# Attention stage of a three-part kernel: third key buffers, an exponential in another place, zero rows written after the first gated tile, maxima turned by a transposition

## The chip, the cores and the metric

The kernel runs on one core of a Trainium2 chip. That core has five engines that run their own instruction streams and meet by semaphores: TensorE (PE, matrix products; PEld is its weight load), VectorE (DVE), ScalarE (ACT), GpSimd (POOL) and SyncE (SP), which here only issues DMA transfers. The metric is the device time of one execution in microseconds, lower is better.

## The reference

Three parts follow each other; the output of one is the input of the next. All values are fp32, and the kernel keeps that accuracy by splitting an operand into a rounded high part and the rest.

```python
# 1: attention, batch 4, 8 heads, 576 positions, 64 wide
scores = q @ k.T / sqrt(64);  cum = cumsum(log(clip(f, 1e-4, 1)))
scores = where(causal, -1e9, scores + cum[:, None] - cum[None, :])
attn = exp(scores - max(scores));  attn /= sum(attn) + 1e-9
x = (attn @ v), heads side by side            # 2304 x 512
# 2: gated product
x = (((x @ w1) * (x @ w2)) @ w3) @ w_out      # 512 -> 1024 -> 1024 -> 512
# 3: one of 8 experts for each row
logits = x @ w_gate;  e = argmax(logits)
gate = softmax(logits)[e];  eom = sigmoid(x @ w_output_gate)
out[rows of e] = gate * eom[e] * (relu(x @ w1[e]) @ w2[e])
```

## The kernel before

Attention goes by 16 tiles of two heads each (four batches of four pairs). A tile passes through some 55 small stages: load of queries, keys and values (`lq`, `lk`, `lv`), rounding of both to a high part on ScalarE (`qh`, `kh`, line 212), the rest of both on VectorE (`ql`, `kl`, line 219), scores from the high parts alone (`X0` to `X3`, `XL`, line 226) for the row maxima on VectorE (`m0` to `mL`, line 261), the turn of the maxima from a column into a row (`Tm`, line 270), its copy (`tc`) and its spread over partitions by two DMA transfers (`mv`, tile MR), the exact scores in four groups A to D (`GA` to `HD`), the exponentials (`eA` to `eD`, line 300), causal masks and sums on GpSimd (`a0` to `s3`, lines 306 and 318), the product with the values (`p0` to `p3`, line 327), the row sums (`su`) and the output copy (`xa`). Rows of the cumulated decay (tile CK) come by DMA (`ck`), and the sums go to DRAM, are inverted there by batches and are read back as a broadcast (`xl`, tiles rb).

The order of all this is written out by hand. `START` gives each stage a time within the tile, `PERIOD` (9.8) the distance of two tiles, `SHIFT` exceptions for single tiles; all (stage, tile) pairs are sorted by that time, and instructions are recorded in that order. Each engine then takes its own in that order and waits where something is not ready. The numbers set an order only, no times. So in one stretch of time stages of three or four tiles are mixed: while GA to GD of tile n run, the values' product is that of tile n - 1, and the first scores are those of tile n + 2. All loads and stores of the stage stand on one queue, SP's.

Between the attention stages, the steps `c0` to `c6` convert weights of the second part (`Combined.narrow`, lines 474 to 492: load, one op on ScalarE, three on VectorE, a rounding on ScalarE, a subtraction on GpSimd). PSUM has three two-bank buffers for all score tiles (`pss`), which rotate; a product waits until its buffer's last reader is through.

The third part scatters each row of its input into a DRAM table `xs`, 2304 rows for each expert; before, 384 rows of each expert must have been cleared (`cr`, line 381), since not all of them are written. In the second part, tile 0 of 512 rows goes through `gated(0)`; then rows of tile 1 are split (`xsplit(1)`), the gates' weights (wg) are loaded, and `project(0)` follows, whose gates' product reads wg (line 682) and whose rows are scattered by GpSimd (line 738).

Lines that matter below:

```python
zt = st["zt"] = p3.tile([P, DM + 2], F32, name="zero", bufs=1)   # tile 2 of attention
SP.dma_start(out=xs[e * N:e * N + W]..., in_=...)                # tiles 4 to 11, one expert each
PE.matmul(s["t"], Ms[s["n"] % 2], ident, start=True, stop=True)  # line 270
SP.dma_start(out=wg[:, :, :2 * E], in_=gates)                    # line 823
```

Of the kernel before, what the change touches and what calls it, by code (L numbers as in the profile page):

```python
# [11 lines left out]
F32 = mybir.dt.float32  # L12
F32R = mybir.dt.float32r
# [10 lines left out]
NP = H // 2  # L24
N = B * S
DM = H * D
FF = 1024
E = 8
P = 128
# [3 lines left out]
W = 3 * P  # L33
# [14 lines left out]

PERIOD = 9.8
START = {  # L50
# [8 lines left out]
}  # L59
SHIFT = {(0, "qd"): -2.0, (0, "lq"): 7.41, (1, "lk"): 0.5, (1, "lq"): 0.5, (0, "XL"): -4.55, (0, "mL"): -5.9, (0, "Tm"): -1.8, (0, "tc"): -1.8, (0, "mv"): -3.49, (1, "Tm"): -0.1, (1, "tc"): -0.1}  # L60

FILL = {(0, "XL"): 10, (1, "X0"): 1, (0, "HA"): 1, (0, "HB"): 3, (1, "XL"): 3, (2, "X0"): 2}

# [7 lines left out]
def spread(nc, d, rz):  # L71

    for h in range(2):
        nc.sync.dma_start(out=d[64 * h:64 * h + 64], in_=rz[h:h + 1].broadcast_to([64, rz.shape[1]]))


def attention(nc, tc, ident, xT, rz, xs, wc, q, k, v, f):
# [6 lines left out]
    V, A, G, PE, SP = nc.vector, nc.scalar, nc.gpsimd, nc.tensor, nc.sync  # L84
    with (
# [7 lines left out]
        p2 = inputs.enter_context(tc.tile_pool(name="at2", bufs=2, side="right"))  # L93
# [22 lines left out]
        CKs = [p1.tile([P, 640], F32R, name=f"CK{i}") for i in range(3)]  # L116
        MRs = [p1.tile([P, S], F32R, name=f"MR{i}") for i in range(2)]
        OQ, OD = p1.tile([P, P], F32R, name="OQ"), p1.tile([P, P], F32R, name="OD")
        KHs = [[p2.tile([P, 640], F32R, name=f"{x}{i}", bufs=1) for i in range(2)] for x in ("kh", "kl")]
        QDs = [p1.tile([P, P], F32R, name=f"QD{i}") for i in range(2)]  # L120
        Ms = [p1.tile([P, 64], F32, name=f"M{i}") for i in range(2)]
        tri, tril = p1.tile([P, 640], F32, name="tri"), p1.tile([P, S], F32, name="tril")
# [57 lines left out]
        st = {}  # L180

        def tl(s, key, shape, dt=F32, bufs=2):
            if key in ("kh", "kl"):
                s[key] = KHs[key == "kl"][s["n"] % 2]
                return s[key][:, :S]
            if key not in s:
                pool = p2 if key in ("qr", "kr", "kh", "kl", "qh", "ql") else p3
                s[key] = pool.tile([P, *shape], dt, name=f"{key}_{s['n']}", tag=key, bufs=bufs)
            return s[key]
# [4 lines left out]
        def load(s, x):  # L194
            n = s["n"]
            src, shape = {"q": (q, (S,)), "k": (k, (S,)), "v": (v, (5, P))}[x]
            SP.dma_start(out=tl(s, x + "r", shape), in_=src[n // NP, n % NP])

        def decay(s):
            n = s["n"]  # L200
# [10 lines left out]
        def high(s, x):  # L211
            A.activation(out=tl(s, x + "h", (S,), F32R), in_=s[x + "r"], func=ACTF.Copy)
# [54 lines left out]
        def turn(s):  # L267
            x = st[s["n"] + 1]["x", 1][:, 256:] if 1 < s["n"] < B * NP - 1 else s["x", 4][:, 896:]
            s["t"] = x[0:64, :P]
            PE.matmul(s["t"], Ms[s["n"] % 2], ident, start=True, stop=True)  # L270

        def turned(s):
            A.activation(out=tl(s, "mt", (P,), F32R)[0:9], in_=s["t"][0:9], func=ACTF.Copy)
# [104 lines left out]
                else:  # L378
                    G.tensor_tensor(out=xT[:, i, 0:512], in0=xT[:, i, 0:512], in1=d, op=ALU.mult)

        def clear_rows(s):

            e = s["n"] - 4
            if e == -2:
                zt = st["zt"] = p3.tile([P, DM + 2], F32, name="zero", bufs=1)
                G.memset(zt, 0.0)
                G.memset(zt[:, DM + 1:], float(2 * N))
            if 0 <= e < E:
                SP.dma_start(out=xs[e * N:e * N + W].rearrange("(c p) d -> p c d", p=P), in_=st["zt"].unsqueeze(1).broadcast_to([P, W // P, DM + 2]))

        stages = {
            "ck": (decay,), "qd": (last_queries,), "XL": (scores_last,), "mL": (maxima, 4), "Tm": (turn,), "tc": (turned,), "mv": (spread_maxima,),
            "p0": (pv, (0,)), "p1": (pv, (1, 2)), "p3": (pv, (3, 4)), "su": (sums,), "xa": (weighted,), "sa": (keep_sums,),
            "zs": (store_sums,), "rl": (invert, 0), "ra": (invert, 1), "rv": (invert, 2), "rs": (invert, 3), "cr": (clear_rows,), "xl": (first_tile, 0), "xm": (first_tile, 1),
        }
        for x in "qkv":
            stages["l" + x] = (load, x)
# [11 lines left out]
        for n in range(B * NP):  # L409
            st[n] = {"n": n}  # L410
        order = [(START[x] + SHIFT.get((n, x), 0.0) + PERIOD * n, n, i, x) for n in range(B * NP) for i, x in enumerate(START)]
        order = sorted(order + [(t + PERIOD * (B * NP - 1), B * NP, 0, x) for x, t in AFTER.items()])
# [132 lines left out]
def moe(nc, tc, ident, xT, rz, xs, xpool, raws, region, wc, w1, w2, gates, e1, e2, out):  # L545

    V, A, G, PE, SP = nc.vector, nc.scalar, nc.gpsimd, nc.tensor, nc.sync
    NCH = N // P
    with (
# [5 lines left out]
        st = {"work": wc.work, "unit": 1}  # L555
# [10 lines left out]
        def tmp(name):  # L566
            return st["work"].tile([P, 512], F32, name=name, tag="tmp", bufs=TMP if "moa" in st else 3)

        def split(src, hi, lo, lo_eng):
            G.tensor_scalar(out=hi, in0=src, scalar1=1.0, scalar2=1.0, op0=ALU.mult, op1=ALU.mult)  # L570
            lo_eng.tensor_tensor(out=lo, in0=src, in1=hi.bitcast(F32), op=ALU.subtract)
# [11 lines left out]
        def xparts(t):  # L583
            return [st["moa"].tile([P, 4, 512], F32R, name=f"{x}{t}", tag=x) for x in ("xh", "xl")]

        def xsplit(t, w, x, ks=range(4)):
            xh, xl = x
            for k in ks:
                xv = xT[:, k, 512 * t:512 * t + w]
                if t:  # L590
                    d = tmp(f"rz{t}{k}")[:, :w]
                    spread(nc, d, rz[k, :, 512 * t:512 * t + w])
                    G.tensor_tensor(out=xv, in0=xv, in1=d, op=ALU.mult)  # L593
                if t:
                    split(xv, xh[:, k, :w], xl[:, k, :w], V)
                else:
                    A.activation(out=xh[:, k, :w], in_=xv, func=ACTF.Copy)
                    V.tensor_tensor(out=xl[:, k, :w], in0=xv, in1=xh[:, k, :w].bitcast(F32), op=ALU.subtract)
# [190 lines left out]
        for hf, j in wc.steps:  # L789
# [4 lines left out]
            if hf and j == 5:  # L794
                wc.first.close()
                st["moa"] = xpool.enter_context(tc.tile_pool(name="moa", bufs=1, side="right", reuse_waits="tile"))
                x = xparts(0)
# [18 lines left out]
        gated(0, TT[0], x, iter(()))  # L816
        x = xparts(1)
        xsplit(1, TT[1], x)


        wg = p1.tile([P, 4, 32], F32, name="wg")
# [26 lines left out]
        with tc.manual_schedule(engines={PE_E, POOL_E}):  # L848
            for t, w in list(enumerate(TT))[1:]:
# [3 lines left out]
                if t + 1 < len(TT):  # L853
                    x = xparts(t + 1)
# [295 lines left out]
        with tc.manual_schedule(engines={PE_E, DVE_E}):  # L1150
# [40 lines left out]
            x = next(fx)  # L1191
# [12 lines left out]
            for i in range(1, E):  # L1204
# [18 lines left out]
                x = next(fx, None)  # L1223
# [9 lines left out]
                else:  # L1233
                    x = turned_piece("p", g2)
                    take(y)
                    p = piece("p", ws2, g2, x)
# [8 lines left out]
        with tc.For_i(1, npieces, 1) as s:  # L1245
            e = nc.values_load(tab[0:1, bass.ds(s + E, 1)], engines=SPE, min_val=0, max_val=E - 1)
# [58 lines left out]
```

## Time and profile before

| | us |
|---|---|
| median of 3 runs | 792.49 |
| lowest, highest run | 791.95, 793.69 |
| profiled execution | 791.35 |
| its span, first to last instruction | 789.7 |
| TensorE busy in the span | 769.1 (97%) |
| VectorE busy | 447.4 (57%) |
| GpSimd busy | 315.9 (40%) |
| ScalarE busy | 280.2 (35%) |

Attention takes the first 173 us or so, the combination of w3 with w_out and the gated product the time to 550 us, the experts the rest. The granted clock of TensorE is 0.996 of full speed as a mean. A row of the timeline gives start, duration, engine, line, operation, and the tiles written and read (buffer numbers left out); in brackets stands how long the engine was idle just before, and what ended that. SPq is SP's instruction stream: its rows are the issues of transfers, not their data. A TensorE row's end is modelled, since matmuls overlap.

### The profile page before, as it was taken

The numbers are of one execution on the slowest core, as the hardware profiler recorded it, in microseconds if no ns is written. First come the engines' busy times: TensorE is split into PE (matmuls) and PEld (weight loads), VectorE is DVE, ScalarE is ACT, GpSimd is POOL, SyncE is SP. The second block draws the span as 40 slices with busy tenths as digits, with TensorE's granted clock in tenths as the row PEclk, the third lists the DMA queues.
The fourth block names the chain that finished last, engine by engine and source line by source line (L and its number), as shares of the span: only waits on it lengthen the run. The fifth ranks groups of instructions, "written<-read, shape, count | busy, mean of one in ns | idle before, by whom it ended". The sixth has DMA issues, their size and how long they took to land. (4 is left out here: it accounts for less than half of the span.)

```text
span 789.7 us, 13796 instructions
## 1 busy us (share of the span) xinstructions
PE 769.1 (97%) x5142; PEld 646.0 (82%) x5142; DVE 447.4 (57%) x982; ACT 280.2 (35%) x542; POOL 315.9 (40%) x343
## 2 busy tenths in 40 slices
PE   7999999999999999999999999999999999999995
PEld 3677777777888887887888788898797999999983
DVE  7689988978989604332350422347468735545620
ACT  3566666654556222212212221214221222322221
POOL 6679999991000501130230111033454444545420
PEclk9999999999999999999999999999999999999998
DMA  3557777534643111010100000054677456456460
GB/s 97 175 164 234 233 234 238 148 115 140 194 152 134 54 42 41 27 40 15 54 16 4 35 27 0 14 169 139 214 240 227 145 204 226 136 189 214 142 268 30
DMA packets 40211, 102.12 MB, mean 129 GB/s; under 512 B 8610, under 2 KB 9314, under 8 KB 39888
## 3 DMA queue, kind: packets, MB, share of 16 engines
q1 hardware_dynamic: 36960, 91.46, 36.0%
q0 software_dynamic: 3184, 9.77, 3.2%
q8 instruction: 41, 0.67, 0.3%
q14 instruction: 26, 0.21, 0.1%
HBM read 84.47 MB, written 16.51 MB: 128 GB/s over the span
## 5 line engine op out<-in xcount | busy, mean ns | idle before, releaser
L607 DVE TENSOR_TENSOR ga<-b,ga 128x512 f32<-128x512 f32 (+1 forms) x40 | 25.4, 635 | 144.4 <-PE b L579 143.7
L738 POOL DMA_INDIRECT xs<-xr,pos x18 | 19.5, 1083 | 174.3 <-DVE pos L732 126.6
L261 DVE CUSTOM_DVE_ANT_0 junk<-x,tri 128x256 f32<-128x256 f32 (+3 forms) x128 | 62.8, 491 | 15.0 <-PE x L226 5.5
L577 PE MATMUL h<-gh,ah 128*128 128x320 f32 (+4 forms) x224 | 67.2, 300 | 0.0
L578 PE MATMUL h<-gl,ah 128*128 128x320 f32 (+4 forms) x224 | 66.9, 299 | 0.0
L579 PE MATMUL h<-gh,al 128*128 128x320 f32 (+4 forms) x224 | 66.9, 299 | 0.0
L577 PE MATMUL b<-xh,w2h 128*128 128x512 f32 (+1 forms) x160 | 59.9, 375 | 0.0
L577 PE MATMUL a<-xh,w1h 128*128 128x512 f32 (+1 forms) x160 | 59.8, 374 | 0.0
L579 PE MATMUL a<-xh,w1l 128*128 128x512 f32 (+1 forms) x160 | 58.9, 368 | 0.0
L579 PE MATMUL b<-xh,w2l 128*128 128x512 f32 (+1 forms) x160 | 58.9, 368 | 0.0
L578 PE MATMUL a<-xl,w1h 128*128 128x512 f32 (+1 forms) x160 | 58.8, 368 | 0.0
L578 PE MATMUL b<-xl,w2h 128*128 128x512 f32 (+1 forms) x160 | 58.8, 368 | 0.0
L577 PE MATMUL y<-raw,gh 128*128 128x512 f32 x144 | 56.8, 395 | 0.0
L579 PE MATMUL y<-raw,gl 128*128 128x512 f32 x144 | 56.2, 390 | 0.0
L578 PE MATMUL y<-raw,gh 128*128 128x512 f32 x144 | 56.0, 389 | 0.0
L609 ACT ACTIVATE gh<-ga 128x512 fp32r<-128x512 f32 (+1 forms) x40 | 23.5, 589 | 89.3 <-DVE ga L607 89.3
L570 POOL TENSOR_SCALAR bh<-rb 128x1024 fp32r<-128x1024 f32 x28 | 35.9, 1283 | 46.1 <-DMA rb<-e 40.6
L1031 DVE SCALAR_TENSOR_TENSOR hl<-h,hh 128x320 fp32r<-128x320 f32 (+4 forms) x56 | 25.5, 462 | 47.9 <-ACT hh L1030 47.2
L593 POOL TENSOR_TENSOR xT<-xT,rz 128x512 f32<-128x512 f32 (+1 forms) x16 | 21.4, 1336 | 78.0 <-DVE ga L607 78.0
L327 PE MATMUL v<-PT,vr 128*64 128x448 f32 (+4 forms) x384 | 52.4, 394 | 0.0
L306 POOL TENSOR_SCALAR_AFFINE_SELECT PT<-PT 128x256 f32<-128x256 f32 (+1 forms) x80 | 42.6, 554 | 22.9 <-ACT PT L300 21.2
L318 POOL TENSOR_TENSOR ac<-ac,PT 128x640 f32<-128x640 f32 (+1 forms) x32 | 47.7, 1490 | 1.6
(617 smaller groups left out, 2120.7 us busy)
## 6 DMA issues: line engine op xcount, KB each, us to landing
ra<-e SPq DMA_DIRECT2D x28, 512.0 KB
rb<-e SPq DMA_DIRECT2D x28, 512.0 KB
w<-w3t SPq DMA_DIRECT2D x16, 512.0 KB
xs<-zero SPq DMA_DIRECT2D x8, 771.0 KB
vr<-v SPq DMA_DIRECT2D x16, 320.0 KB
kr<-k SPq DMA_DIRECT2D x16, 288.0 KB
qr<-q SPq DMA_DIRECT2D x16, 288.0 KB
wo<-wo SPq DMA_DIRECT2D x8, 512.0 KB
```

The costliest lines, as they stand in the source:

```text
L261: V.tensor_tensor_reduce(out=junk[:, :w], in0=s["x", i][:, 512 * h:512 * h + w] if i < 4 else s["x", i][:, 224:224 + S], in1=tri[:, 640 - ...
L306: G.affine_select(out=t, in_=t, pattern=[[0, 2], [1, w]], compare_op=ALU.is_ge, fill=0.0, base=0, channel_multiplier=-1,)
L318: G.tensor_tensor(out=acc[:, :, q0 - P:], in0=first if j == 1 else acc[:, :, q0 - P:], in1=src, op=ALU.add)
L327: PE.matmul(s["v"][HALF[h], 384 + q0:384 + q1], s["vr"][:, j, HALF[h]], place(s, j, h, q0, q1), start=(j == 0), stop=(j == 4 or q1 == P),)
L570: G.tensor_scalar(out=hi, in0=src, scalar1=1.0, scalar2=1.0, op0=ALU.mult, op1=ALU.mult)
L577: PE.matmul(ps, ah, bh, start=start and i == 0, stop=False)
L578: PE.matmul(ps, ah, bl, start=False, stop=False)
L579: PE.matmul(ps, al, bh, start=False, stop=stop and i == last)
L593: G.tensor_tensor(out=xv, in0=xv, in1=d, op=ALU.mult)
L607: V.tensor_tensor(out=ga[:, :w], in0=pb[:, :w], in1=ga[:, :w], op=ALU.mult)
L609: A.activation(out=gh[:, f, :w], in_=ga[:, :w], func=ACTF.Copy)
L1031: V.scalar_tensor_tensor(out=hl[:, f, :w], in0=ps[:, :w], scalar=0.0, in1=hh[:, f, :w].bitcast(F32), op0=ALU.max, op1=ALU.subtract)
```

## The change

Nothing is computed differently. Six edits:

- The keys' tiles as loaded (kr) and as rounded (kh) have three buffers in place of two. `lk` moves ahead by about 15 units and `kh` by 5, so a tile's keys are loaded and rounded a period earlier than before; `SHIFT` keeps the first tiles near their old places. One more small clearing of a pad goes with the third kh buffer.
- `eD`, the exponential of group D, moves from 13.33 to 12.6, ahead of `qh` of a later tile (12.68 in the same terms).
- `c2`, one of the conversion ops on VectorE (line 483), moves from 2.78 to 1.2, ahead of `kl` and `ql`.
- `xl`, the broadcast of the inverted sums, moves from 33.6 to 36.3.
- The zero rows are no longer written in attention: the clearing of the tile and all eight transfers stand behind `xsplit(1)` of the second part and ahead of the gates' load. The tile is one of the three `raw` buffers there.
- The turn of the maxima is a transposition of TensorE in place of a product with the identity.

```diff
-    "lk": -16.99, "c0": -13.79, "c1": -4.9, "lq": -16.9, "ck": -8.57, "kh": -7.55, "c2": 2.78, "qh": -6.92,
+    "lk": -31.9, "c0": -13.79, "c1": -4.9, "lq": -16.9, "ck": -8.57, "kh": -12.6, "c2": 1.2, "qh": -6.92,
...
-    "HD": 11.31, "a0": 11.0, ... "c3": 13.19, "eD": 13.33, "c4": 13.3, ...
+    "HD": 11.31, "a0": 11.0, ... "c3": 13.19, "eD": 12.6, "c4": 13.3, ...
-    "p3": 25.66, "su": 26.2, "xl": 33.6, ...
+    "p3": 25.66, "su": 26.2, "xl": 36.3, ...
-SHIFT = {(0, "qd"): -2.0, (0, "lq"): 7.41, (1, "lk"): 0.5, (1, "lq"): 0.5, ...
+SHIFT = {(0, "qd"): -2.0, (0, "lq"): 7.41, (0, "lk"): 14.91, (1, "lk"): 15.41, (2, "lk"): 14.9, (3, "lk"): 5.8, (4, "lk"): 2.1, (2, "lq"): 0.5, (0, "kh"): 5.05,  (1, "lq"): 0.5, ...
-        KHs = [[p2.tile([P, 640], F32R, name=f"{x}{i}", bufs=1) for i in range(2)] for x in ("kh", "kl")]
+        KHs = [[p2.tile([P, 640], F32R, name=f"{x}{i}", bufs=1) for i in range(c)] for x, c in (("kh", 3), ("kl", 2))]
-            SP.dma_start(out=tl(s, x + "r", shape), in_=src[n // NP, n % NP])
+            SP.dma_start(out=tl(s, x + "r", shape, bufs=3 if x == "k" else 2), in_=src[n // NP, n % NP])
-            PE.matmul(s["t"], Ms[s["n"] % 2], ident, start=True, stop=True)
+            PE.transpose(s["t"], Ms[s["n"] % 2], ident)
-        def clear_rows(s):
-            ...
         xsplit(1, TT[1], x)
+        zt = wc.work.tile([P, DM + 2], F32, name="zero", tag="raw", bufs=3)
+        G.memset(zt, 0.0)
+        G.memset(zt[:, DM + 1:], float(2 * N))
+        for e in range(E):
+            SP.dma_start(out=xs[e * N:e * N + W].rearrange("(c p) d -> p c d", p=P), in_=zt.unsqueeze(1).broadcast_to([P, W // P, DM + 2]))
```

What SP issues at the start, before. kr and qr are keys and queries of one tile as loaded, CK its decay rows, MR its spread maxima (two transfers), QD the blocks of the last queries:

```order
L197 DMA kr_215<-k 128x576
L197 DMA qr_217<-q 128x576
L192 DMA CK_109<-EK 2x576 x2
L197 DMA kr_269<-k 128x576
L197 DMA qr_271<-q 128x576
L192 DMA MR_111<-mt_276 2x4x128
L192 DMA MR_111<-mt_276 2x1x64
L192 DMA QD_120<-qh_273 64x64 x2
L474 DMA wo_303<-wo 128x512
L192 DMA CK_110<-EK 2x576 x2
L209 DMA EKd<-EK 32x576 x2
```

and with the change:

```order
L198 DMA kr_217<-k 128x576
L198 DMA qr_219<-q 128x576
L193 DMA CK_109<-EK 2x576 x2
L198 DMA kr_271<-k 128x576
L193 DMA MR_111<-mt_276 2x4x128
L193 DMA MR_111<-mt_276 2x1x64
L198 DMA qr_280<-q 128x576
L198 DMA kr_282<-k 128x576
L193 DMA QD_121<-qh_273 64x64 x2
L465 DMA wo_307<-wo 128x512
L198 DMA kr_360<-k 128x576
L193 DMA CK_110<-EK 2x576 x2
```

The queries of tile 2 have moved behind the maxima of tile 0, and two more key loads stand ahead of the decay rows of tile 2.

The same queue where the sums of the first batch are read back as a broadcast (rb), in tiles 7 to 9, before. vr are values, zd the stored sums, w a weight of the second part:

```order
L197 DMA kr_1449<-k 128x576
L197 DMA qr_1451<-q 128x576
L354 DMA zd<-zs_1401 2x2x288
L197 DMA vr_1463<-v 128x640
L74 DMA rb_5_1475<-rz 64x512 x2
L192 DMA QD_120<-qh_1454 64x64 x2
L474 DMA w_1508<-w3t 128x512
L192 DMA MR_111<-mt_1498 2x4x128
L192 DMA MR_111<-mt_1498 2x1x64
L389 DMA xs<-zero 128x3x514
L206 DMA CK_109<-EKd 2x576 x2
L197 DMA kr_1607<-k 128x576
```

and with the change:

```order
L198 DMA qr_1449<-q 128x576
L355 DMA zd<-zs_1401 2x2x288
L198 DMA vr_1461<-v 128x640
L193 DMA QD_121<-qh_1452 64x64 x2
L465 DMA w_1502<-w3t 128x512
L193 DMA MR_111<-mt_1492 2x4x128
L193 DMA MR_111<-mt_1492 2x1x64
L74 DMA rb_5_1518<-rz 64x512 x2
L198 DMA kr_1523<-k 128x576
L207 DMA CK_109<-EKd 2x576 x2
L198 DMA qr_1606<-q 128x576
L355 DMA zd<-zs_1559 2x2x288
```

The broadcast has moved from ahead of the maxima to behind them, the zero rows are gone, and the key load stands ahead of the decay rows in place of behind them.

The same queue at the gates' load in the second part, before (rz are broadcasts of the sums for tile 1 and tile 2):

```order
L74 DMA rz_3476<-rz 64x512 x2
L74 DMA rz_3482<-rz 64x512 x2
L74 DMA rz_3488<-rz 64x512 x2
L823 DMA wg<-gates 128x4x16
L74 DMA rz_3978<-rz 64x512 x2
L74 DMA rz_3984<-rz 64x512 x2
```

and with the change:

```order
L74 DMA rz_3467<-rz 64x512 x2
L74 DMA rz_3473<-rz 64x512 x2
L74 DMA rz_3479<-rz 64x512 x2
L814 DMA xs<-zero 128x3x514 x8
L819 DMA wg<-gates 128x4x16
L74 DMA rz_3980<-rz 64x512 x2
```

All eight writes of zero rows stand right ahead of the gates' load.

## Rows read from the trace of the kernel before

**Rows 1.** Busy time by stretch: us from the start, length, engines, granted clock, DMA share, GB/s

```profile
60.00:98.80 38.80, 38.80 (x441) 30.50 (x439) 36.09 (x93) 26.34 (x45) 35.99 (x37) 1.00 0.75 236
98.80:141.30 42.50, 39.72 (x446) 30.98 (x442) 37.48 (x94) 26.72 (x45) 39.55 (x39) 1.00 0.74 235
173.00:300.00 127.00, 127.00 (x620) 102.14 (x619) 89.81 (x159) 57.99 (x104) 19.40 (x20) 1.00 0.37 124
```

**Rows 2.** Timeline of TensorE, the first products gA of tiles 6, 8 and 12

```profile
79.26 0.51 PE L226 MATMUL gA<-qh,kh 64*128 64x192 f32 x4
...
98.80 0.51 PE L226 MATMUL gA<-qh,kh 64*128 64x192 f32 x4
...
141.28 0.51 PE L226 MATMUL gA<-qh,kh 64*128 64x192 f32 x4
```

**Rows 3.** Timeline of all engines within one period

```profile
78.71 1.28 POOL L492 TENSOR_TENSOR cw<-w01u,cw 128x512 fp32r<-128x512 f32 x1
...
79.83 0.79 DVE L219 TENSOR_TENSOR kl<-kr,kh 128x576 fp32r<-128x576 f32 x1
...
80.53 1.57 DVE L219 TENSOR_TENSOR ql<-qr,qh 128x576 fp32r<-128x576 f32 x1
...
83.17 0.68 ACT L212 ACTIVATE kh<-kr 128x576 fp32r<-128x576 f32 x1
...
83.74 0.67 ACT L212 ACTIVATE qh<-qr 128x576 fp32r<-128x576 f32 x1
...
84.44 0.69 ACT L300 ACTIVATE PT<-gD 128x640 f32<-128x640 f32 x1
...
84.65 0.19 PEld L226 LDWEIGHTS x<-kh,qh 64*128 64x128 f32 x2 [0.70 <-ACT z L367]
84.65 0.39 PE L226 MATMUL x<-kh,qh 64*128 64x256 f32 x2
```

**Rows 4.** Waits in 0 to 180 us: who for whom, us, times, longest

```profile
DVE junk L261 <- PE x L226: 5.5, 10, 0.8
```

**Rows 5.** Instructions of line 270: duration ns min/median/max, first and last start

```profile
L270 PE MATMUL x<-ident,M x26: 272/298/324, 36.8 to 158.7; 128*64 128x128 f32 x26
```

**Rows 6.** Timeline of ScalarE, SP and TensorE at the start

```profile
15.76 0.27 ACT L273 ACTIVATE mt<-xl 9x128 fp32r<-9x128 f32 x1 [1.84 <-PE xl L270]
...
17.03 1.15 SPq L192 DMA_DIRECT2D MR<-mt  x2
...
19.79 0.51 PE L226 MATMUL gA<-MR,CK 64*128 64x192 f32 x4 [1.35 <-DMA MR<-mt]
```

**Rows 7.** Timelines of SP, TensorE, GpSimd and VectorE in tiles 8 and 9

```profile
97.14 1.18 SPq L192 DMA_DIRECT2D MR<-mt  x2
...
100.47 0.51 PE L226 MATMUL gA<-MR,CK 64*128 64x192 f32 x4 [0.67 <-DMA MR<-mt]
...
104.44 1.28 POOL L379 TENSOR_TENSOR xT<-xT,rb 128x512 f32<-128x512 f32 x1
...
110.09 1.58 DVE L219 TENSOR_TENSOR kl<-kr,kh 128x576 fp32r<-128x576 f32 x1
```

**Rows 8.** Two zero writes and the gates' load by stretch, the clearing, and timelines

```profile
69.60:71.90 2.30, 2.30 (x34) 2.27 (x36) 2.27 (x6) 2.00 (x4) 2.11 (x3) 1.00 0.92 347
130.80:134.10 3.30, 3.30 (x48) 3.23 (x48) 3.27 (x6) 2.87 (x5) 3.30 (x4) 1.00 0.78 253
278.00:278.70 0.70, 0.70 (x6) 0.57 (x5) 0.30 (x5) 0.07 (x1) 0.00 (x0) 1.00 0.50 47
...
L386 POOL MEMSET zero<- x1: 543/543/543, 38.6 to 38.6; 128x514 f32 x1
...
274.85 0.94 POOL L570 TENSOR_SCALAR xh<-xT 128x512 fp32r<-128x512 f32 x1
...
276.73 0.58 SPq L823 DMA_DIRECT2D wg<-gates  x1
...
296.76 1.06 PE L682 MATMUL lt<-xT,wg 128*32 128x512 f32 x8
```

More of the change, by code (lines that the diff above doesn't have):

```diff
@@ L50 @@
 START = {
[1 row of a table removed]
[1 row of a table added]
     "X1": -5.99, "m1": -5.27, "X3": -5.12, "X2": -5.07, "m3": -2.49, "X0": -1.58, "m2": -1.5, "m0": -1.24, "qd": -4.8,
[1 row of a table removed]
[1 row of a table added]
     "HA": 8.43, "GB": 8.46, "HB": 8.5, "GC": 8.77, "HC": 9.64, "eA": 10.17, "eB": 10.24, "eC": 11.25, "GD": 11.28,
[1 row of a table removed]
[1 row of a table added]
     "s1": 13.9, "a2": 14.0, "s2": 14.5, "c6": 17.0, "s3": 17.5, "p0": 22.91, "p1": 24.73,
[1 row of a table removed]
[1 row of a table added]
     "rs": 48.4,
 }
-SHIFT = {(0, "qd"): -2.0, (0, "lq"): 7.41, (1, "lk"): 0.5, (1, "lq"): 0.5, (0, "XL"): -4.55, (0, "mL"): -5.9, (0, "Tm"): -1.8, (0, "tc"): -1.8, (0, "mv"): -3.49, (1, "Tm"): -0.1, (1, "tc"): -0.1}
+SHIFT = {(0, "qd"): -2.0, (0, "lq"): 7.41, (0, "lk"): 14.91, (1, "lk"): 15.41, (2, "lk"): 14.9, (3, "lk"): 5.8, (4, "lk"): 2.1, (2, "lq"): 0.5, (0, "kh"): 5.05,  (1, "lq"): 0.5, (0, "XL"): -4.55, (0, "mL"): -5.9, (0, "Tm"): -1.8, (0, "tc"): -1.8, (0, "mv"): -3.49, (1, "Tm"): -0.1, (1, "tc"): -0.1}
 FILL = {(0, "XL"): 10, (1, "X0"): 1, (0, "HA"): 1, (0, "HB"): 3, (1, "XL"): 3, (2, "X0"): 2}
@@ L183, in tl @@
             if key in ("kh", "kl"):
-                s[key] = KHs[key == "kl"][s["n"] % 2]
+                ring = KHs[key == "kl"]
+                s[key] = ring[s["n"] % len(ring)]
                 return s[key][:, :S]
@@ L379, in first_tile @@
                     G.tensor_tensor(out=xT[:, i, 0:512], in0=xT[:, i, 0:512], in1=d, op=ALU.mult)
-        def clear_rows(s):
[L383 to L389, printed above, removed]
         stages = {
@@ L393, in attention @@
             "p0": (pv, (0,)), "p1": (pv, (1, 2)), "p3": (pv, (3, 4)), "su": (sums,), "xa": (weighted,), "sa": (keep_sums,),
-            "zs": (store_sums,), "rl": (invert, 0), "ra": (invert, 1), "rv": (invert, 2), "rs": (invert, 3), "cr": (clear_rows,), "xl": (first_tile, 0), "xm": (first_tile, 1),
+            "zs": (store_sums,), "rl": (invert, 0), "ra": (invert, 1), "rv": (invert, 2), "rs": (invert, 3), "xl": (first_tile, 0), "xm": (first_tile, 1),
         }
```

6 rows, old and new, of the table START are left out of this document.

## The prediction

> **What bounds the kernel now.** I read the table by stage first, then the order of starts on TensorE, then one tile's period engine by engine, and last the two places that the change touches from outside: the start, and the gates' first use. In the table the reader is to see that from 173 us on TensorE is busy 127.00 of 127.00 us [rows 1], so a microsecond won or lost in attention arrives at the end whole. In attention nothing is idle long either: in 60 to 98.8 us TensorE shows 38.80, VectorE 36.09 and GpSimd 35.99 of 38.8 us; in 98.8 to 141.3 us GpSimd has 39.55 of 42.5 [rows 1].
>
> The work goes by tiles of two heads, and I count a period from the first product gA of one tile to that of the next. From 79.26 to 98.80 two periods take 9.77 us each; from 98.80 to 141.28 four take 42.48 [rows 2], which is 42.48 - 4 x 9.77 = 3.40 us more than four of the usual ones. That is the largest sum that the profile offers.
>
> Inside a usual period the loop goes through two engines. ScalarE rounds keys (kh, 0.68 us), then queries (qh, 0.67), then takes the fourth exponential (0.69); TensorE stands 0.70 us at the first score product until qh is there [rows 3]. (The row names the small op z, which ran right behind qh in this period.) VectorE waits for those same products ten times, 5.5 us together [rows 4], about half a microsecond each, the longest 0.8.
>
> **The change, part by part.**
>
> *Fourth exponential ahead of the queries' rounding, keys' rounding a tile earlier.* kh leaves the place ahead of qh (0.68 us) and the exponential takes it (0.69): qh ends 0.01 us later, so the first score product starts when it did. kh goes to where ScalarE waits for TensorE's row sums, ahead of the output copy. What the exponential gives back is its PSUM bank, which the second score product needs: it ended at 84.44 + 0.69 = 85.13, and the products that start at 84.65 take 0.39 us alone [rows 3], so at most 0.1 us, and VectorE's next step does not depend on it. I count 0.
>
> *Conversion step c2 ahead of the keys' low part.* VectorE's kl took 0.79 us at 79.83, when GpSimd's subtraction (78.71 + 1.28 = 79.99) was just ending, and ql took 1.57 from 80.53, when the next sum on GpSimd was running [rows 3]; kl took 1.58 at 110.09 [rows 7]. So an op with two inputs in SBUF waits for the GpSimd op that it meets: 0.79 is the price of one such wait. Now c2 stands first and kl meets what ql met before, ql meets the causal masks instead. One wait moves from ql to kl; the row ends about where it did. Bounds: one wait less or half a wait more in some 12 periods, read as -0.2 to +0.4 us each, so -2.4 to +4.8; I take 0, since the number of meetings is the same.
> The Trainium skill (SBUF — State Buffer, Who interferes with whom) says that VectorE and GpSimd lock each other out for a whole instruction, and that `tensor_scalar`, which c2 is, can take that lock as well; the pair 0.79 and 1.58 agrees with a full wait. By that rule c2 in front adds a holder ahead of kl; it is the second of the slower rivals below.
>
> *Keys in third buffers.* The load of a tile's keys no longer waits for the last but one tile, and on the SP queue it moves ahead of the decay rows (CK) and the queries. At the start this frees the copy of the row maxima: it was ready at 15.76 + 0.27 = 16.03, was issued at 17.03 behind the keys and queries of tile 2, and TensorE began with it at 19.79, having stood 1.35 us [rows 6]. Now queries follow the maxima, so up to 1.0 us is won there. But the next such copy has only what the SP queue leaves: a key load now stands at VectorE's kl before CK and the store of the decay rows. I keep 0.4 of 1.0; bounds 0 and -1.0.
> A load that waits for kl on SP holds CK back in every period: kl ends at 80.62, the score product that starts at 84.65 uses CK 0.2 us later [rows 3]. Even with kl one wait (0.79) later, at 81.4, with 1.0 for both issues and 1.3 from an issue to its data (the gates' issue at 276.73, their data from 278.0 [rows 8]), CK comes at 83.7; the keys' own 288 KB are through by then (81.4 + 1.3, and 0.8 at 347 GB/s [rows 8]: 83.5). About one microsecond is left, less where a store of the sums stands in between.
>
> *Zero rows and the sums' broadcast leave the path of the maxima.* In the period from 98.80 the maxima were issued at 97.14, TensorE stood 0.67 us for them at 100.47 [rows 7] and the period after was long as well: GpSimd's extra product of 1.28 us (104.44) made it late, and kl met it (1.58 instead of 0.79) [rows 7]. The broadcast of the sums stood on SP before the queries' blocks, the weights' load and the maxima; it now comes behind the maxima. What can come back of the 3.40: GpSimd was busy 39.55 of these 42.5 us [rows 1], so no more than 42.5 - 39.6 = 2.9; and at least one of the two waits for the maxima, 0.7. I take 1.6, since GpSimd takes part of the wait back: the multiplication was partly hidden behind it. A like broadcast in the period after 141.28 gives 0.3 more. Together -1.9, bounds -0.7 and -3.4.
>
> *Maxima transposed.* The product with the identity is two passes of 272 to 324 ns each, 26 in the group shown and six more at the ends for 16 tiles [rows 5]; as a transposition it is one. They overlap the value products behind them, so a pass costs TensorE between nothing and 0.1 us: 0 to -1.6 in all. I take -0.3. The copy of the maxima comes up to 0.15 us sooner, which counts only where TensorE waits for it.
>
> *Zero rows written later.* Eight writes of 771 KB are 6.32 MB. One of them alone filled a window at 347 GB/s, another at 253 [rows 8]: 18.2 us or 25.0 for eight. They start behind GpSimd's last split (274.85 + 0.94) and its clearing of the tile (0.54, and 0.1 for its last column): 276.4 [rows 8]. The gates' load, issued at 276.73 before, is now behind them on the same queue. With 1.3 us from issue to data: 276.4 + 1.3 + 18.2 = 295.9, and 0.7 more for the gates (their data filled 278.0 to 278.7 [rows 8]): 296.6. TensorE needs the gates at 296.76 [rows 8]. So the cover is 20 us of products, all but used up; at 253 GB/s it ends at 303.4 and TensorE stands 6.6 us. Bounds 0 and +6.6; I take +0.5, near the faster row: the slower window has the DMA engines busy 0.78 of its time against 0.92, so it is a tail in which some engines had run out, and of eight writes in a row only the last has such a tail.
> The Trainium skill (DMA: Bandwidth & Descriptors, Specifications) gives about 358 GB/s to and from HBM for one core; 347 agrees with it, 253 does not. By that figure the writes are an estimated 17.6 us, and nothing stands.
>
> **Sum.** -0.4 (start) - 1.9 (maxima on time) - 0.3 (one pass) + 0.5 (gates) = -2.1. The profiled execution took 791.35 us, 789.7 in its span; the median of the runs is 792.49, 1.1 above it. The same 2.1 taken from the median gives 790.4.
>
> **Rivals.**
> 1. *More comes back.* Period 98.80 to 141.28 falls to GpSimd's floor (-2.9), the start keeps all (-1.0), one pass gives 0.1 a tile (-1.6): with the rest -5.8, 786.7. For it: TensorE's 0.67 at 100.47. Against: GpSimd's 39.55 busy.
> 2. *The maxima are still not on time, or GpSimd keeps what they give.* The 1.9 falls to 0.3, the gates take 0.5: about -0.4, 792.1, no change. For it: GpSimd 93% busy there. Against: a wait of TensorE for a transfer whose issue is moved ahead.
> 3. *Slower: the gates wait behind the zeros.* At 253 GB/s +6.6 against the other -2.6: +4.0, 796.5. Decided by the drain: from 18.4 us on it costs, and from 21 us on it eats the whole gain. For it: the window at 253 GB/s. Against: the idle share in that same window.
> 4. *Slower: c2 in front makes kl and ql wait once more.* +0.4 in 12 periods, +4.8 - 2.1 = +2.7, 795.2. It decides as soon as VectorE's idle time before the score maxima (5.5 us in ten waits) is used up. For it: kl's 1.58. Against: ql's wait that it replaces.
>
> **How the numbers follow.** Forecast 0.50 (789.0 to 791.8), rival 1 0.15, rival 2 0.17, rival 3 0.10, rival 4 0.08. About 0.2%, 1.6 us, is what a measurement of this kernel can tell from no change: faster is below 790.9, slower above 794.1. Two thirds of the forecast's own range and rival 1 lie below: 0.50 with a little of rival 2; slower 0.20 with a tail of 2; the rest, 0.30, is the same. The range 787.0 to 794.5 leaves out rival 3 and the far half of rival 1.
>
> **What would show it.** Right: a period of 9.7 to 9.8 in 60 to 98.8 us; the four periods behind it in 40.5 to 41.3 without a wait of TensorE for the maxima; gA's last part of tile 0 at 18.8 instead of 19.79; the first gates product within 1 us of the product before it. Wrong: a wait of TensorE for the gates of 2 us or more; usual periods above 10 us, with VectorE's kl or the CK rows as the releaser; or the four periods at 42 as before.

## The result, and the profile after

The changed kernel takes 796.43 us (median of 7 runs, 795.0 to 800.69) beside 791.53 for the kernel before: ratio 1.0067, interval 1.0048 to 1.0085, so 3.8 to 6.7 us slower. The forecast was 790.4, range 787.0 to 794.5. The profiled execution took 795.65 us, 794.0 in its span, 4.3 more than the span of before. Of these 4.3, 1.6 are there when attention ends (tile 15's first gA starts at 171.04, before at 169.44), 1.8 come at the gates, and the rest is spread over what follows.

The table by stretch of the changed kernel (columns as in [rows 1]):

```profile
60.00:98.80 38.80, 38.57 (x418) 28.52 (x416) 34.46 (x91) 26.32 (x45) 34.35 (x36) 1.00 0.50 144
98.80:141.30 42.50, 39.50 (x436) 29.11 (x434) 37.01 (x92) 26.22 (x45) 37.47 (x39) 1.00 0.51 157
173.00:300.00 127.00, 125.41 (x624) 101.51 (x620) 90.62 (x156) 57.62 (x104) 19.88 (x23) 1.00 0.53 175
```

GpSimd falls from 39.55 to 37.47 us in the second stretch, so here its busy time is not what holds the four long periods; and TensorE no longer fills 173 to 300 us. The starts of tiles 6, 8 and 12, on TensorE:

```profile
79.91 0.51 PE L227 MATMUL gA<-qh,kh 64*128 64x192 f32 x4
...
100.01 0.51 PE L227 MATMUL gA<-qh,kh 64*128 64x192 f32 x3
...
143.04 0.36 PE L227 MATMUL gA<-qh,kh 64*128 64x192 f32 x2
```

Two usual periods take 20.10 us instead of 19.54, the four behind them 43.03 instead of 42.48 [rows 2]. Who waits, on TensorE in 17 to 173 us, first before, then changed (waiting op, what for, us in all, times, longest):

```profile
PE gA L226 <- DMA MR<-mt: 4.1, 5, 1.3
```

```profile
PE gA L227 <- DMA MR<-mt: 3.5, 2, 1.8
PE x L227 <- DMA CK<-EKd: 1.2, 2, 0.9
```

Five waits for the maxima have become two that are longer, and the decay rows are waited for, which did not happen in this stretch before. The first long one is in tile 1 (ScalarE, SP, TensorE):

```profile
16.36 0.27 ACT L274 ACTIVATE mt<-xl 9x128 fp32r<-9x128 f32 x1 [1.63 <-PE xl L271]
```

```profile
19.02 0.41 PE L227 MATMUL gA<-MR,CK 64*128 64x192 f32 x4
...
31.49 0.51 PE L227 MATMUL gA<-MR,CK 64*128 64x192 f32 x4 [1.79 <-DMA MR<-mt]
```

```profile
27.59 0.58 SPq L465 DMA_DIRECT2D w<-w3t  x1
28.27 1.16 SPq L193 DMA_DIRECT2D MR<-mt  x2
```

Tile 0's maxima, copied by 16.63 and issued at 16.66, came in time, against a wait of 1.35 [rows 6]; tile 1's then cost 1.79 us. Their transfer was issued 0.68 us behind a weight block of 512 KB, whose packets moved from 28.79 to 30.90; the maxima's moved at 30.64, 2.4 us behind their issue. The second is in tile 8, the same picture:

```profile
97.11 0.54 SPq L465 DMA_DIRECT2D w<-w3t  x1
97.85 1.18 SPq L193 DMA_DIRECT2D MR<-mt  x2
99.09 1.13 SPq L74 DMA_DIRECT2D rb<-rz  x2
```

```profile
102.75 0.51 PE L227 MATMUL gA<-MR,CK 64*128 64x192 f32 x4 [1.74 <-DMA MR<-mt]
```

Nothing was late on SP: the issue came at 97.85, at the end of the copy it needs, and the broadcast rb stood behind it as the change wants. But the maxima's packets (512 bytes each) moved only at 101.50 to 101.67, when the block's 4096-byte packets (98.50 to 101.56) were all but through. That is 3.65 us behind the issue; in tiles 14 and 15, with no block ahead, they move 1.2 us behind it. (The broadcast's first packets, issued behind the maxima, moved at 100.47 already, so the packets of one queue did not start strictly in the order of issue.)

The wait for the decay rows, in tile 11, on VectorE, SP and TensorE:

```profile
133.04 1.84 DVE L220 TENSOR_TENSOR kl<-kr,kh 128x576 fp32r<-128x576 f32 x1
```

```profile
134.90 0.33 SPq L198 DMA_DIRECT2D kr<-k  x1
135.29 0.64 SPq L372 DMA_DIRECT2D rz<-z  x1
136.03 0.72 SPq L207 DMA_DIRECT2D CK<-EKd  x2
```

```profile
138.66 0.56 PE L227 MATMUL x<-CK,OQ 64*128 64x256 f32 x2 [0.87 <-DMA CK<-EKd]
```

The key load is issued only when VectorE's kl has ended (134.88), then a store of the sums goes, then CK.

At the zero rows, on SP, TensorE and VectorE:

```profile
278.02 10.01 SPq L814 DMA_DIRECT2D xs<-zero  x8
288.13 1.78 SPq L819 DMA_DIRECT2D wg<-gates  x1
```

```profile
300.20 1.18 PE L673 MATMUL lt<-xT,wg 128*32 128x512 f32 x8 [1.79 <-DMA wg<-gates]
```

```profile
300.07 0.21 DVE L726 COPY xr<-tof 128x1 f32<-128x1 f32 x2 [20.23 <-DMA rz<-rz]
300.20 0.69 DVE L598 TENSOR_TENSOR ga<-b,ga 128x512 f32<-128x512 f32 x1
```

TensorE stands 1.79 us for the gates. VectorE stands too: at 300.07 it copies row numbers into a row tile, with the gated product's ga queued behind. The row names the broadcasts rz, but rz's packets end at 301.72, after the copy. What ended just before are the zero rows: their packets run from 278.95 to 299.37. For the row tile of rows 512 and on, the ring of three `raw` buffers has come round to the one that held the zeros, so its first writer waits until all eight writes have read it (the run `z_dep` below takes this wait away).

### The profile page after: what moved, and what is told of

Same layout as the page of the kernel before. It is cut to its first block, busy times and chain, and to the rows that moved or that the text cites. A ratio compares the mean times of both kernels' runs of the same rounds, so it can differ in the third digit from the quotient of the medians.

```text
span 794.0 us, 13739 instructions
## 1 busy us (share of the span) xinstructions
PE 770.6 (97%) x5126; PEld 639.8 (81%) x5126; DVE 448.1 (56%) x983; ACT 279.5 (35%) x542; POOL 309.3 (39%) x343
## 5 line engine op out<-in xcount | busy, mean ns | idle before, releaser
L729 POOL DMA_INDIRECT xs<-xr,pos x18 | 19.4, 1076 | 174.6 <-DVE pos L723 128.5
L584 POOL TENSOR_TENSOR xT<-xT,rz 128x512 f32<-128x512 f32 (+1 forms) x16 | 19.8, 1234 | 77.3 <-ACT w2h L481 77.3
L328 PE MATMUL v<-PT,vr 128*64 128x448 f32 (+4 forms) x384 | 49.8, 396 | 0.0
L319 POOL TENSOR_TENSOR ac<-ac,PT 128x640 f32<-128x640 f32 (+1 forms) x32 | 44.3, 1384 | 1.6
```

Of the source, the lines that this page charges most:

```text
L319: G.tensor_tensor(out=acc[:, :, q0 - P:], in0=first if j == 1 else acc[:, :, q0 - P:], in1=src, op=ALU.add)
L328: PE.matmul(s["v"][HALF[h], 384 + q0:384 + q1], s["vr"][:, j, HALF[h]], place(s, j, h, q0, q1), start=(j == 0), stop=(j == 4 or q1 == P),)
```

## The experiments

Every ratio is to the kernel before, timed beside it on the same chip; 0.001 is 0.8 us.

**Undoing one part of the change.**

Gates first (`u_gates`):

```diff
+        SP.dma_start(out=wg[:, :, :2 * E], in_=gates)
         for e in range(E):
             SP.dma_start(out=xs[e * N:e * N + W]..., in_=zt...)
-        SP.dma_start(out=wg[:, :, :2 * E], in_=gates)
```

> The changed kernel with one edit: the eight writes of zero rows are issued behind the gates' load instead of ahead of it. Theory: in the changed kernel TensorE stood 1.79 us at its first gates' product for that load, and nothing else of this stage is on the path, so about 1.8 us come back of the 4.9 lost: some 794.6 beside 791.5 for the kernel before (ratio 1.004), and the first gates' product follows without a wait. Rival: the zero writes then hold up the transfers behind them (broadcasts of the sums, the first scatter at 308), and the wait only moves: time as the changed kernel's, 796.4 (1.0062).

Ratio 1.0055 (1.0036 to 1.0075), not told apart from 1.0067, nor from the theory's 1.004: here the trace decides. On TensorE, VectorE and TensorE's clock (columns of the last as in [rows 1]; the clock is the third number from the end):

```profile
299.04 1.06 PE L673 MATMUL lt<-xT,wg 128*32 128x512 f32 x8
...
305.94 0.66 PE L678 MATMUL lg<-ident,lp 128*128 128x128 f32 x4 [2.88 <-ACT lp L675]
```

```profile
303.91 0.21 DVE L726 COPY xr<-tof 128x1 f32<-128x1 f32 x2 [23.36 <-DMA rz<-rz]
304.05 0.69 DVE L598 TENSOR_TENSOR ga<-b,ga 128x512 f32<-128x512 f32 x1
```

```profile
306.00:308.00 2.00, 2.00 (x10) 1.68 (x11) 1.35 (x8) 0.60 (x2) 0.00 (x0) 0.80 0.02 8
308.00:310.00 2.00, 2.00 (x6) 1.58 (x5) 1.72 (x17) 0.20 (x1) 0.00 (x0) 0.50 0.47 123
```

The gates' product runs without a wait, but VectorE's copy stays until the zero rows are through, ScalarE's lp stands behind ga, and TensorE waits 2.88 us for lp. Behind this stop the granted clock fell to 0.50, the lower of its two levels. So the wait moved, though not to the broadcasts or the scatter that the rival named.

Key loads at their old place, with SHIFT's entries for lk and lq as before (`u_lk`), and c2 (`u_c2`):

```diff
-    "lk": -31.9,
+    "lk": -16.99,
```

```diff
-    "c2": 1.2,
+    "c2": 2.78,
```

> The changed kernel with one edit: the key loads go back to where they stood on the SP queue before the change (behind the decay rows CK, beside the queries); third buffers, the earlier rounding of keys and all else stay. Theory: the early key load stands on SP at VectorE's subtraction kl and bunches CK, queries, values, weights and maxima behind it; TensorE's waits for CK (1.2 us in the trace, two in a third tile) go and the waits for the maxima (3.5 us in two tiles) shrink to 1.5 or less: 3 us come back, about 793.4 (ratio 1.0024). Rival: the loss in attention is VectorE's own, from c2 ahead of kl and ql; then less than 0.5 us comes back, 796 (1.0057).

> The changed kernel with one edit: c2 back behind kl and ql on VectorE. Theory (key loads are the cause): kl still ends when it did in half of the tiles, since it meets GpSimd's product itself, but where c2 took 1.1 to 1.3 us kl ends up to 0.4 sooner and so does the key load that waits for it: 0.5 to 1 us come back, 795.6 (1.0052). Rival (c2 is the cause): usual periods go back to 9.77 us and 2 us or more come back, 794.3 or less (1.0035).

1.0071 (1.0047 to 1.0094) and 1.0050 (1.0032 to 1.0068): neither is told apart from the change. In the trace of `u_lk` the waits for CK are gone, as expected, but those for the maxima are 4.8 us in five tiles, and the clock fell to 0.52 in 22 to 24 us. While such waits and drops are left, a single part can't be told apart from the change.

**The zero rows alone.** The kernel before with the writes moved behind the gates' load (`d_zeros`):

```diff
-    "cr": 7.59,
...
+        zt = wc.work.tile([P, DM + 2], F32, name="zero", tag="raw", bufs=3)
...
         SP.dma_start(out=wg[:, :, :2 * E], in_=gates)
+        for e in range(E):
+            SP.dma_start(out=xs[e * N:e * N + W]..., in_=zt...)
```

> The kernel before with one edit: the clearing of the tile and the eight writes of zero rows are moved out of attention, behind the gates' load. Theory: the maxima's transfers of tiles 8, 10 and 12 no longer stand behind zero writes and come on time; TensorE's waits for them there (about 0.7, 0.7 and 0.3 us) go, GpSimd takes part back: 1 to 1.5 us faster than before, 790.3 (0.9985). Rival: GpSimd's product of the first tile, not the transfers, sets these four periods, and nothing changes: 791.5 (1.000).

1.0015 (0.9996 to 1.0034). The starts of tiles 8 and 12:

```profile
101.09 0.36 PE L226 MATMUL gA<-qh,kh 64*128 64x192 f32 x2
...
143.32 0.35 PE L226 MATMUL gA<-qh,kh 64*128 64x192 f32 x2
```

Four periods take 42.23 us against 42.48 [rows 2]: the zero rows had hardly held the maxima up. Next to nothing changes there, as the rival said; that GpSimd is the reason is not shown. VectorE's stop is in this run too (its copy starts at 301.85), but TensorE stood only 0.83 us for lp behind it.

Both waits at the zero rows taken away: the copy of the row numbers takes the gate value as a second operand, so it can't stand early in VectorE's queue. Without gates first (`z_dep0`), with it (`z_dep`), on the kernel before (`d_dep`), and with the key loads back as well (`z_dep_lk`):

```diff
-                V.tensor_copy(xr[:, DM + 1:DM + 2], tof[:, ...])
+                V.scalar_tensor_tensor(out=xr[:, DM + 1:DM + 2], in0=z[:, c:c + 1], scalar=0.0, in1=tof[:, ...], op0=ALU.mult, op1=ALU.add)
```

> The changed kernel with one edit: the copy of the row numbers into the row tiles (line 726) takes the gate value as a second operand, times zero, so that it can't be recorded before the gate value is there; the gates' load stays behind the zero writes. In the runs before, VectorE stood at this copy for tile 1's rows until the last zero write was through (to 300.0 us in the changed kernel, 303.7 with the gates' load in front), since their buffer is the one that held the zeros, and the gated product's ga was queued behind. Theory: each of the two waits alone holds TensorE; this takes away one, so the gates' wait of 1.8 us stays and the time is the changed kernel's, ratio 1.006. Rival: VectorE's stop is the whole cost, and some 2 us come back, ratio 1.0035.

> The same edit of the copies, and the gates' load ahead of the zero writes. Theory: both waits are gone, TensorE runs through 290 to 320 us without a stop, and 1.8 us of the profile, with what a drop of the clock behind such a stop cost in other executions up to 3, come back: ratio 1.003, some 2.5 us above the kernel before, which is what attention loses. Rival: the drain costs by its traffic alone and the time stays at ratio 1.005 or more.

> The kernel before with the zero writes moved to the same late place, gates' load first, and the same edit of the copies: the part of the change that was meant to relieve the maxima, without its two waits. Theory: tiles 8 to 13 gain 0.25 us as in the run with the zero writes moved alone (42.23 against 42.48 us), so the time is that of before, ratio 0.9995. Rival: the maxima gain the 1 to 2 us that the prediction counted, ratio 0.998.

> The run without both waits, and the key loads back to their old place on SP. Theory: the waits of TensorE for the decay rows (1.2 to 1.4 us in the changed kernel's traces, none with the key loads back) go, and nothing else changes: 0.8 to 1.2 us faster than the run without both waits, ratio 1.0015. Rival: the earlier maxima of tile 0, which the key loads' place had freed, are lost again and cancel it: the same ratio as that run.

`z_dep0` 1.0090 (1.0074 to 1.0105): the gates' wait alone holds TensorE (2.51 us in its trace), as VectorE's stop alone does in `u_gates`. It is not faster than the change; the granted clock is part of that: four of its five runs have a mean of 0.990 to 0.993, and the fifth, at 0.995, took 795.12 us. `z_dep` 1.0020 (1.0003 to 1.0037): 0.0047 below the change, 3.7 us, come back when both are gone. VectorE's ga then waits only for its own product:

```profile
298.23 0.69 DVE L598 TENSOR_TENSOR ga<-b,ga 128x512 f32<-128x512 f32 x1 [18.67 <-PE b L570]
```

`d_dep` 1.0003 (0.9990 to 1.0016): moving the zero rows without a wait gives nothing by itself. `z_dep_lk` 0.9998 (0.9987 to 1.0009), 0.0022 below `z_dep`: the early key loads cost some 1.7 us here. The two intervals overlap a little, but the two kernels were timed beside each other, twelve runs each, and their means differ by 1.9 us (95% interval 0.5 to 3.2). Part of it is the clock: the mean granted is 0.994 with the early key loads and 0.996 without.

**What stands ahead of the maxima.** The weight block's load, which the change left in its place, moved behind them: on the kernel before (`d_c0`), on `z_dep` (`z_dep_c0`) and on `z_dep_lk` (`z_dep_lk_c0`). Beside them the transposition alone on the kernel before (`d_tr`).

```diff
-    "c0": -13.79,
+    "c0": -12.95,
```

> The kernel before with one edit: the load of a weight block (w, wo; 256 KB) is issued behind the maxima's two transfers instead of right ahead of them. Theory: on the one queue the maxima's packets land only when the block ahead of them is nearly through (issue to data 1.4 to 2.3 us with it, 1.2 in tiles 14 and 15 where no block stands ahead), so each of TensorE's waits for the maxima (4.1 us in five tiles) shrinks by 0.4 to 0.6: 2 to 2.5 us faster, ratio 0.997. Rival: what delays the maxima is the list of keys, queries and values ahead of the block, or GpSimd takes back what they give: ratio 0.999 to 1.

> The changed kernel without its two waits at the zero rows, and the weight blocks' load behind the maxima. Theory: the two long waits for the maxima in the changed kernel's attention (2.0 us each in tiles 1 and 8, where the list behind the key load has the block go out right ahead of the maxima) fall to 1 or less, and with them some of the clock's drops behind them: 2 to 3 us faster than without this edit, ratio 0.999. Rival: they come from SP being late with the maxima themselves, and nothing changes: ratio 1.002.

> The same with the key loads back at their old place. Theory: neither the decay rows nor the maxima are waited for in usual tiles; the fastest of all, 2 us below the kernel before, ratio 0.9975. Rival: the weight block now meets the decay rows and keys instead, which moves the wait to them: ratio 1.000 as without this edit.

> The kernel before with the transposition alone. Theory: the turn takes one pass instead of two (0.30 us where it was 0.43 from first start to last end), the copy of the maxima ends about 0.15 sooner, and TensorE's five waits for them shrink by that at most, if the queue lets them through: 0 to 0.8 us faster, ratio 0.9995. Rival: a pass less is worth 0.1 us of TensorE in every tile besides: 1.6 us, ratio 0.998.

(The block has 512 KB by the profile's list of issues, not 256, and the two long waits are 1.79 and 1.74 us, not 2.0.) `z_dep_c0` 0.9971 (0.9960 to 0.9982) and `z_dep_lk_c0` 0.9963 (0.9949 to 0.9978): faster than the kernel before, as the theory said. SP and TensorE in tile 8 of `z_dep_c0`, then TensorE's waits in `z_dep` and in `z_dep_c0`:

```profile
95.30 1.18 SPq L193 DMA_DIRECT2D MR<-mt  x2
96.58 0.34 SPq L465 DMA_DIRECT2D w<-w3t  x1
96.97 1.14 SPq L74 DMA_DIRECT2D rb<-rz  x2
```

```profile
98.29 0.41 PE L227 MATMUL gA<-MR,CK 64*128 64x192 f32 x4
```

```profile
PE gA L227 <- DMA MR<-mt: 2.9, 3, 1.7
```

```profile
PE x L227 <- DMA CK<-EKd: 0.4, 1, 0.4
...
PE gA L227 <- DMA MR<-mt: 0.2, 1, 0.2
```

The maxima's packets move 1.2 us behind their issue in every tile, where `z_dep` has 1.8 to 2.9 us in the tiles with a block ahead, and the waits for them are 0.2 us in place of 2.9. On the kernel before the same edit is a loss, 1.0063 (1.0046 to 1.0080), against both expectations. TensorE's waits there:

```profile
PE x L226 <- DMA CK<-EKd: 5.6, 6, 1.1
PE gA L226 <- DMA MR<-mt: 2.4, 3, 1.3
```

The waits for the maxima shrink, but behind them now stand the block, a zero write of 771 KB and only then CK: 5.6 us of waits for CK take their place. With the zero writes moved late as well (`d_dep_c0`, below) no wait for CK is left in this stretch, only

```profile
PE gA L226 <- DMA MR<-mt: 1.7, 2, 1.3
```

This is what the zero rows' move is worth: nothing alone, but it makes room for the block. `d_tr` 1.0007 (0.9993 to 1.0021): no gain from one pass.

**The sizes, on a quiet base.** With late maxima gone, or all but gone, the runs of one kernel lie within 0.6 to 2.7 us, of `a_c0` within 4.2 (of the changed kernel 5.7), so smaller terms can show. The changed kernel with the block behind the maxima and nothing else (`a_c0`); then `z_dep_lk_c0` with the turn as a product again (`b_mm`), c2 back (`b_c2`), the broadcast back at 33.6 (`b_xl`), and with tile 2's keys and queries behind tile 0's maxima (`b_start`, the diff below); last, the kernel before with late zero rows as in `d_dep` and the block behind the maxima (`d_dep_c0`).

```diff
+SHIFT = {..., (2, "lk"): 0.5, (2, "lq"): 0.5, ...}
```

> The changed kernel with one edit: the weight blocks' load behind the maxima. Its two waits at the zero rows (gates' load behind them, VectorE's copy into the buffer that held them) stay. Theory: the waits for the maxima in attention are half of what the change loses, the zero rows the other half; beside the run without those two waits (ratio 0.997) this is 1.8 to 2.8 us slower, ratio 0.9995 to 1.001. Rival: the zero rows cost more than the profile's 1.8 us in most executions, through the clock: ratio 1.003.

> The fastest version so far (key loads back, both waits at the zero rows taken away, weight blocks behind the maxima; ratio 0.9963) with one edit: the turn of the maxima as a product with the identity again. Theory: the maxima have slack now in usual tiles, so that 0.15 us later changes nothing there, and a pass more costs TensorE 0 to 0.1 us in some tiles: 0 to 0.5 us slower, ratio 0.9965. Rival: a pass is 0.1 us in every tile: 1.6 us, ratio 0.998.

> The same fastest version with one edit: c2 back behind kl and ql. Theory: in tiles 9 to 13, where GpSimd has its extra products, VectorE meets GpSimd as often either way: no change, ratio 0.9963. Rival: c2 in front makes kl and ql wait once more (1.83 and 1.57 us in tiles 9 and 11), and taking it back gives 0.5 to 1 us in these five tiles: ratio 0.9955.

> The same fastest version with one edit: the broadcast of the sums back to where it stood, ahead of the queries' blocks and the maxima. Theory: its 256 KB then delay the maxima of tiles 8, 10 and 12 by 0.5 to 1 us of the wait, but the product that uses it meets GpSimd no earlier: 1 to 2 us slower, ratio 0.998. Rival: the maxima have slack enough, and nothing changes: ratio 0.9963.

> The kernel before with two edits and none of the change's others: the zero rows written late without the two waits (gates' load first, the row numbers' copy bound to the gate value), and the weight blocks' load behind the maxima. Each of the two alone gave nothing or a loss (ratio 1.0003 and 1.0063). Theory: together they are the whole gain of the fastest version, since the zero rows no longer push the decay rows when the block stands behind the maxima: ratio 0.9965. Rival: the rounding of keys a tile earlier and the exponential's place carry part of it: ratio 0.998 or more.

> The fastest version (key loads back, no waits at the zero rows, weight blocks behind the maxima) with one edit: at the start the keys and queries of tile 2 are loaded behind tile 0's maxima instead of ahead of them. Theory: TensorE's last wait for the maxima, 1.1 to 1.3 us in tile 0, goes, and 0.4 us of it stays won at tile 1 as in the run with the early key loads (27.98 against 28.35): ratio 0.9958. Rival: tile 2's scores come later by as much: no change, 0.9963.

| kernel | ratio | interval |
|---|---|---|
| `a_c0` | 1.0017 | 1.0006 to 1.0028 |
| `b_mm` | 0.9960 | 0.9946 to 0.9973 |
| `b_c2` | 0.9966 | 0.9953 to 0.9980 |
| `b_xl` | 0.9959 | 0.9947 to 0.9972 |
| `d_dep_c0` | 0.9962 | 0.9946 to 0.9978 |
| `b_start` | 0.9956 | 0.9941 to 0.9972 |

`a_c0`, between its theory and its rival, is 0.0046 above `z_dep_c0`: the waits at the zero rows cost 3.6 us, as much as between the change and `z_dep`. Its own trace shows 2.1 us of waiting for the gates. Undoing a part (`b_mm`, `b_c2`, `b_xl`) can't be told from 0.9963, for `b_xl` against its theory, and `d_dep_c0`, which has none of the change's other parts, is as fast as `z_dep_lk_c0`: the gain is the block and the zero rows together, as far as these intervals can tell. `b_start` has no wait for the maxima left and the lowest ratio, but 0.9956 is not told apart from 0.9963.

## Why the prediction was wrong

Three steps failed. The forecast was 2.1 us below the kernel before, the changed kernel came 5.3 above it (ratio 1.0067). The zero rows, counted at +0.5, cost 3.6 to 3.7; the key loads ahead of CK, counted at nothing, cost some 1.7; and the -1.9 for the maxima did not come: without the first two (`z_dep_lk`) the time is that of before, 0.9998. Of the prediction's own signs of being wrong, the four periods did not shorten (43.03 us), usual ones took 10.05 us each, though without a wait of TensorE for CK between tiles 6 and 8, and the gates' wait, 1.79 us, stayed just below its 2. Rival 3 names 796.5, all but the measured 796.43, but by luck: its sum is +6.6 for the gates and -2.6 of gains, and neither came.

*Maxima on time, -1.9: did not come.* It took the broadcast and the zero rows for what holds the maxima up, because they stood on the queue around them. `d_zeros` gave 0.25 us of it, taking back the broadcast's move (`b_xl`) cost nothing that can be told, and with both moved and the block still ahead (`z_dep_lk`) the four periods take 42.15 us (99.19 to 141.34) against 42.48. What held them was the weight block, which the change left right ahead of them: the prediction followed when SP issues and not when packets move. With the block moved, the four periods from tile 8 take 41.05 us in `z_dep_lk_c0` (97.42 to 138.47), within the 40.5 to 41.3 that was forecast, but by an edit that the change does not have. GpSimd is busy 39.83 of these 41.05 us, so the floor that the prediction set by GpSimd may hold; no run tested it.

*Gates behind the zeros, +0.5: the largest miss, mis-sized and in part overlooked.* The place was right. The drain took 20.4 us (278.95 to 299.37), not 18.2, and the gates landed at 299.60; rival 3 lets a drain cost from 18.4 us on, so 20.4 make 2.0, and 1.79 came. The table by stretch:

```profile
278.90:290.00 11.10, 11.10 (x54) 9.20 (x53) 0.63 (x8) 2.30 (x6) 0.29 (x1) 1.00 1.03 371
290.00:299.40 9.40, 8.41 (x41) 6.60 (x39) 0.00 (x0) 2.30 (x6) 0.00 (x0) 1.00 1.03 301
```

The rate was 371 GB/s at first, above both windows of [rows 8], and 301 in the second part. Seven of the eight writes' packets were through by 293.94, some 2.1 us for each write; the last write's took 5.4 us more, and in these the gates and the broadcasts moved as well (from 295.98). So only the last write has a tail, as was argued, but its length was counted at next to nothing. The Trainium skill (DMA: Bandwidth & Descriptors, Specifications) gives about 358 GB/s, by which nothing would have stood; the trace goes above it and below it, and the measurement decides. The overlooked part is VectorE's stop: the text names the tile's clearing but does not ask who takes its buffer next. Both waits together cost 3.6 to 3.7 us by the ratios. From tile 15's first gA to the last instruction the four traces with both waits (the changed kernel, `u_lk`, `u_c2`, `a_c0`) take 623.0 to 624.0 us, the ten with late zero rows and neither wait 620.5 to 622.5: 2.5 us as a mean. The other microsecond is within what the intervals leave open; a drop of the clock behind the stop, seen in the trace of `u_gates`, may be part of it.

*Start, -0.4.* Tile 0's wait went, as said, and tile 1's grew from 0.96 to 1.79 us behind the block. By tile 3 the changed kernel is 0.28 us later than before, of which 0.73 were lost ahead of the first product (18.18 against 17.45): the size is about right in this trace, and too small to be timed.

*Key loads and CK.* "About one microsecond is left, less where a store of the sums stands in between" was right on the place: tile 11 waits behind just such a store. Counting it as nothing was wrong: CK's waits are 1.2 us in the trace, and the early key loads with all that queues behind them cost 1.7 in `z_dep` against `z_dep_lk`. With the block moved the two differ by no more than the intervals allow (0.9971 and 0.9963).

*One pass, -0.3.* One of the two passes goes (in tile 0 the turn takes 0.30 us where it took 0.43), and no gain can be told: `d_tr`, `b_mm`. *c2, 0.* Right in time. In half of the tiles c2 itself meets GpSimd's sum (1.26 us at 90.43, beside 0.42 to 0.52 in others) and kl then takes 0.74: the wait changes hands, as was argued; rival 4 did not come (`u_c2`, `b_c2`). *eD and kh, 0.* Nothing can be told of them either: `d_dep_c0`, without them, is as fast.

## What to carry to other kernels

Here a small transfer that an engine waits for moved 1.2 us behind its issue with nothing large right ahead of it, and 1.4 to 3.7 us behind it with a 512 KB block there: order a queue by what is waited for, put bulk behind, and look at what then stands behind the bulk (`d_c0`). When a buffer is lent to a long run of transfers, look up which later instruction takes it next, and what that engine has queued behind. Test small edits after the big waits are gone; before that they could not be told apart here.

## What the runs showed of the hardware

The same stop of TensorE can be followed by a drop of its clock or not: in `d_zeros` a wait of 1.26 us at 19.73 was followed by a granted clock of 0.69 and 0.50 (the lower level) in the next two stretches of 2 us, while the kernel before stood 1.35 us at the same place [rows 6] at a full clock behind it:

```profile
20.00:22.00 2.00, 2.00 (x15) 1.08 (x13) 1.93 (x8) 1.30 (x2) 0.62 (x2) 0.69 0.70 176
22.00:24.00 2.00, 2.00 (x9) 1.12 (x9) 0.52 (x1) 0.32 (x1) 0.79 (x1) 0.50 0.54 176
```

Twelve of the traces have a wait of 1.0 to 1.4 us for the maxima of tile 0, at 19.4 to 19.8. In five of them (`d_zeros`, `u_lk`, `d_tr`, `b_mm`, `b_c2`) the drop follows, and tile 1's first gA starts at 29.8 to 30.1; in the other seven it does not follow, and it starts at 28.3 to 28.6. None of the eight traces without the wait has a drop there. So the same wait has two prices, some 1.5 us apart, which is as much as some of the parts that are told apart above; what decides between them is not shown. The seven runs of the changed kernel show it too: mean clock 0.997 at 795.0 us and 0.990 at 800.69; with most waits gone, `z_dep_lk_c0` lies within 788.84 to 790.05.
